# Reordering the opening of a two-layer convolution and feed-forward kernel, and splitting its last store

## The chip, the cores and the metric

One core of a Trainium2 chip, each group of runs on one chip. The engines are named as the profile names them: PE does the matmuls (PEld its weight loads), DVE is the vector engine, ACT the scalar engine, POOL the GpSimd engine, and SP the engine that issues most transfers (DMA); PSUM is the memory into which PE writes its results. The time is the device time of one launch in microseconds (us); a row of runs is given by its median. The profile's span is shorter than the time by a constant 1.8 us or so (353.4 against 355.2 for one run of the kernel before). A few runs of such kernels fall in a slower state, with a lower granted clock; all runs used here are of the fast state unless said otherwise. The kernel before took 355.32 us (354.15 to 355.44) before any of this.

## The reference, cut to what matters

```python
def A(q, k, v, shift_k, ssm_k, ssm_D):          # long convolution, S = 2048, D = 512
    k_shift = causal 4-tap filter of k per column, taps shift_k
    kv = k_shift * v
    y  = irfft(rfft(kv, 2S) * rfft(ssm_k, 2S))[:S]
    return q * (y + kv * ssm_D)
def B(x, w_gate, w_up, w_down):                 # F = 1792
    return (silu(x @ w_gate) * (x @ w_up)) @ w_down

x = q
for layer in range(2):
    x = x + A(layernorm(x), k, v, ...)
    x = x + B(layernorm(x), ...)
```

## The kernel before

The rows are cut into four chunks of 512. The Fourier transforms are matmuls with tables of sines (`fwd`, `inv`), `h` is the convolution's kernel `ssm_k`, and the four-tap filter is a matmul of the transposed `k` (`kTb`) with diagonal matrices of the taps (`dg`). One chunk's convolution runs among the feed-forward matmuls of the chunk ahead of it. To that end every operation is first put on a list, with engine, estimated cost and buffers; a planner orders the list, and the program is then emitted in that fixed order. An engine runs its own operations strictly in that order.

```python
SLK = 9.39                                      # constants that steer the planner; some 15 of them, tuned together
ST1 = lambda l, c, h: (l, c, h) in {(0, 2, 0), (0, 3, 1), (1, 0, 1)}   # which statistics go to ACT
...
def add(self, eng, cost, emit, r=(), w=(), lat=None, due=None, ...):   # one operation for the planner
...
    for o in seq:                                # emission, in the planned order
        ...                                      # warming matmuls fill the planned wait at the start:
        n = int((start - t - 0.4) / 0.085)
        o.emit()
...
    load_k(0, -70)                               # on ACT
    ... tapR ...                                 # on SP
    load_h(0, "ACT", -59)                        # second on ACT
    load_v(0, -59); load_x(0, -58)               # on SP
    # a tiny copy makes the gate weights wait for h:
    add("POOL", 0.1, lambda: nc.gpsimd.tensor_copy(out=wt["g"].t[0:1, 0, 0:1], in_=hn[0].t[0:1, 0, 0:1]), ...)
    wg = load_weights("g", -57)
    load_h(1, "SP", -56.5, after=[wg]); load_k(1, -56.4, after=[wg])
    load_weights("u", -56, after=[wg]); load_weights("d", -55, after=[wg])
    ...
    for n in range(2):                           # inverse tables: 14 PE transposes, 2 ACT copies
        for i in range(NI):
            nc.tensor.transpose(it.t[:, i, :], fwd.t[:, n * NI + i, :], ident.t[:])
    ...
    v1 = load_v(1, ...)                          # the second chunk's v, on SP, into the one buffer of the first
```

## Time and profile before

| | before |
|---|---|
| first useful matmul | 7.18 us |
| first feed-forward matmul | 35.94 us |
| end of the last matmul | 350.11 us |
| end of the span | 353.4 us |
| PE waits after the first useful matmul | 0.2 us, once |

A feed-forward matmul is one with `pf` or `pd` as output. The time can be read as three stretches: up to the first useful matmul; the opening, from there to the first feed-forward matmul; and the main part, to the last matmul. In the last two PE works almost without a break (the view of waits leaves out gaps under 0.15 us). The view of waits for PE of the kernel before has one entry besides the start (engine, output, line, what it waited for: total us, times, longest us):

```profile
PE pf L335 <- ACT sg L838: 0.2, 1, 0.2
```

The second `v` was issued at 24.81 us, landed 8.0 us later, and the first product with it ran on DVE at 41.7 us.

### The profile page before, as it was taken

Reading aid. Unit: us, or ns where it says so; the run is one execution under the profiler, and the core shown is the slowest. Engines: PE = TensorE matmul, PEld = TensorE weight load, DVE = VectorE, ACT = ScalarE, POOL = GpSimd, SP = SyncE. Lnnn points to the kernel's source line nnn. Section 1 sums busy time; section 2 is a strip of 40 time slices with the busy share of each in tenths; the row PEclk is TensorE's granted clock in tenths of the full one; section 3 lists DMA queues with packets and bytes.
Section 4 is the critical chain, followed back from the end, with each engine's and each line's share of the span. In section 5 each row is a group of like instructions: output and inputs, shape, how many; then the busy total and the mean of one; then the engine's idle time right before and its main releaser. Section 6 shows DMA issues by size and latency. Waiting matters only on the chain.

```text
span 353.4 us, 6784 instructions
## 1 busy us (share of the span) xinstructions
PE 347.8 (98%) x2716; PEld 254.9 (72%) x2716; DVE 276.4 (78%) x511; ACT 249.6 (71%) x470; POOL 38.2 (11%) x42
## 2 busy tenths in 40 slices
PE   7999999999999999999999999999999999999996
PEld 7745976867777686858677676758687777778673
DVE  4997999999989999999997999799973323545111
ACT  4768684859897865758869994946488975646452
POOL 1001010111102110111220010201111000001000
PEclk9999999999999999999999999999999999999999
DMA  6999230010343222012101033010101010101100
GB/s 238 289 340 312 49 88 3 2 30 2 71 109 76 77 89 32 0 32 60 32 32 31 14 107 61 0 32 1 32 30 32 30 32 1 24 7 24 37 2 30
DMA packets 37897, 21.98 MB, mean 62 GB/s; under 512 B 29797, under 2 KB 35690, under 8 KB 37866
## 3 DMA queue, kind: packets, MB, share of 16 engines
q1 hardware_dynamic: 37192, 20.51, 22.0%
q10 hardware_dynamic: 674, 1.05, 0.9%
q8 instruction: 21, 0.34, 0.4%
q14 instruction: 10, 0.08, 0.1%
HBM read 12.33 MB, written 2.10 MB: 41 GB/s over the span
## 4 chain that ended last, share of the span: by engine, by line
PE 65%; DVE 26%; ACT 4%; issue 2%; POOL 2%; ACTq 0%; DVEq 0%; POOLq 0%
PE pf L335 36%; PE pd L852 18%; PE ps L335 8%; DVE ht L845 3%; DVE bnst L707 3%; DVE m L519 2%; DVE t L636 2%; DVE t L652 2%; DVE t L642 2%; ACT H L424 2%; DVE Z L657 2%; PE wm L1024 2%; DVE G L556 1%; DVE xc L778 1%; POOL rstd L712 1%
## 5 line engine op out<-in xcount | busy, mean ns | idle before, releaser
L335 PE MATMUL pf<-zT,wg_sb 128*128 128x256 bf16 x896 | 116.1, 273 | 0.2 <-ACT sg L838 0.2
L335 PE MATMUL pf<-zT,wu_sb 128*128 128x256 bf16 x896 | 116.1, 273 | 0.0
L852 PE MATMUL pd<-wd_sb,ht 128*128 128x512 bf16 x448 | 103.1, 379 | 0.0
L335 PEld LDWEIGHTS <-wg_sb 128*128 128x128 bf16 x896 | 87.6, 98 | 19.4 <-issue 0.5
L335 PEld LDWEIGHTS <-wu_sb 128*128 128x128 bf16 x896 | 87.6, 98 | 11.4
L838 ACT ACTIVATE sg<-pf 128x512 bf16<-128x512 f32 x112 | 67.5, 603 | 26.1 <-PE pf L335 25.9
L842 ACT CAST ht<-pf 128x512 bf16<-128x512 f32 x112 | 66.0, 590 | 18.7 <-PE pf L335 18.1
L852 PEld LDWEIGHTS <-ht 128*128 128x128 bf16 x448 | 43.8, 98 | 47.1
L845 DVE TENSOR_TENSOR ht<-ht,sg 128x1024 bf16<-128x1024 bf16 x64 | 39.3, 618 | 33.4 <-ACT ht L842 33.4
L712 POOL TENSOR_TENSOR rstd<-ve,nhalf 128x2 f32<-128x2 f32 x25 | 29.1, 1163 | 207.0 <-DVE ve L710 185.8
L707 DVE BATCH_NORM_STATS2 bnst<-xc 128x6 f32<-128x512 bf16 x50 | 32.2, 683 | 0.5
L864 ACT CAST dn<-pd 128x512 bf16<-128x512 f32 x26 | 13.9, 589 | 25.1 <-PE pd L852 25.1
L636 DVE TENSOR_TENSOR t<-X,G 128x2048 bf16<-128x2048 bf16 x18 | 21.9, 1218 | 0.0
L642 DVE TENSOR_TENSOR t<-X,G 128x2048 bf16<-128x2048 bf16 x18 | 21.9, 1217 | 0.0
L871 DVE TENSOR_TENSOR xc<-xc,dn 128x1024 bf16<-128x1024 bf16 x13 | 8.9, 687 | 15.9 <-ACT dn L864 15.8
L424 ACT ACTIVATE X<-ps 128x512 bf16<-128x512 f32 x32 | 18.6, 605 | 2.0 <-PE ps L335 1.9
L751 ACT ACTIVATE z<-xc,nmr,rstd 128x512 bf16<-128x512 bf16 x18 | 13.6, 807 | 2.7 <-DVE nmr L744 2.6
L737 POOL TENSOR_TENSOR rstd<-ve,nhalf 128x2 f32<-128x2 f32 x7 | 7.8, 1117 | 70.5 <-DVE ve L733 70.5
L335 PE MATMUL ps<-vt,fwd 128*128 128x512 bf16 x56 | 15.2, 379 | 0.0
L335 PEld LDWEIGHTS <-fwd 128*128 128x128 bf16 x96 | 9.3, 98 | 7.9 <-issue 0.2
L652 DVE TENSOR_TENSOR t<-t,t 128x2048 bf16<-128x2048 bf16 x12 | 14.7, 1221 | 0.1
L657 DVE TENSOR_TENSOR Z<-Z,t 128x2048 bf16<-128x2048 bf16 x12 | 14.7, 1221 | 0.1
(96 smaller groups left out, 317.6 us busy)
## 6 DMA issues: line engine op xcount, KB each, us to landing
vt<-in_A_v_dram SPq DMA_DIRECT2D x4, 512.0 KB, 4.0
xc<-in_A_q_dram SPq DMA_DIRECT2D x4, 512.0 KB, 4.9
out_dram<-xc SPq DMA_DIRECT2D x16, 128.0 KB, 1.8
wg_sb<-in_B_w_gate_dram SPq DMA_DIRECT2D x1, 1792.0 KB, 7.7
wu_sb<-in_B_w_up_dram SPq DMA_DIRECT2D x1, 1792.0 KB
wd_sb<-in_B_w_down_dram SPq DMA_DIRECT2D x1, 1792.0 KB, 13.4
hn<-in_A_ssm_k_dram SPq DMA_DIRECT2D x3, 512.0 KB, 6.3
kn<-in_A_k_dram ACTq DMA_DIRECT2D x1, 512.0 KB, 3.5
```

The source lines that it names most:

```text
L335: nc.tensor.matmul(o, lhsT=lhsT, rhs=rhs, start=(n == 0), stop=(n == len(terms) - 1))
L424: add("ACT", act(D), lambda: nc.scalar.activation(out=view(), in_=ps.t[:], func=ACT.Copy, scale=scale), r=[ps], w=[(buf, keys)], conv=conv)
L636: dve(n * D, lambda t1=t1, part=part: nc.vector.tensor_mul(out=t1.t[:], in0=x.t[:, sl, 0, :], in1=g.t[:, sl, part, :]), [(x, key(slots, (0 ...
L642: dve(n * D, lambda t2=t2, part=part: nc.vector.tensor_mul(out=t2.t[:], in0=x.t[:, sl, 1, :], in1=g.t[:, sl, 1 - part, :]), [(x, key(slots ...
L652: dve(n * D, lambda t1=t1, t2=t2, comb=comb: nc.vector.tensor_tensor(out=t1.t[:], in0=t1.t[:], in1=t2.t[:], op=comb), [t2], [t1], conv=conv)
L657: dve(n * D, lambda t1=t1, part=part: nc.vector.tensor_add(out=z.t[:, sl, part, :], in0=z.t[:, sl, part, :], in1=t1.t[:]), [t1], [zk], con ...
L707: add("DVE", 0.6, lambda st=st, i=i: nc.vector.bn_stats(out=st.t[:], in_=xs[c].t[:, i, :]), r=[(xs[c], (i,))], w=[st])
L712: add("POOL", PW, lambda: nc.gpsimd.tensor_tensor(out=rstd.t[:], in0=ve.t[:], in1=nhalf.t[:].to_broadcast((P, n)), op=ALU.pow), r=[ve, nha ...
L838: add("ACT", act(D), lambda ps=ps, o=o, sg=sg: nc.scalar.activation(out=sg.t[:, o:o + 2, :], in_=ps.t[:], func=ACT.Silu), r=[ps], w=[(sg, ...
L842: add("ACT", act(D), lambda ps=ps, o=o, ht=ht: nc.scalar.copy(out=ht.t[:, o:o + 2, :], in_=ps.t[:]), r=[ps], w=[(ht, (o // 2,))], due=(uni ...
L845: dve(n * W, lambda sg=sg, ht=ht: nc.vector.tensor_mul(out=ht.t[:], in0=ht.t[:], in1=sg.t[:]), [sg], [ht], due=(unit, k / pairs, 0.0, "h"))
L852: nc.tensor.matmul(pds[o].t[:], lhsT=ht.t[:, q, o * P:(o + 1) * P], rhs=wt["d"].t[:, ft, :], start=(ft == 0 and not xpe), stop=(ft == NF - 1))
```

## The change

The intent is to start PE's useful work earlier. The first `h` becomes the first transfer of ACT's queue, alone there. The other loads stand in one line on SP, and the gate weights no longer wait for `h`. The filter of `k` is done by column groups, so that it can start on a part; half of the spectrum of `h` comes ahead of it. The statistics and normalisation of the first rows move from DVE to ACT. The inverse tables are made by two transposing DMA loads in place of PE. The last row's result is copied and stored in two halves on two queues. All planner constants were tuned anew. The core of the diff, with cuts:

```diff
-SLK = 9.39
+SLK = 8.59
 ...                                             (all planner constants)
-                            n = int((start - t - 0.4) / 0.085)
+                            n = int((start - max(t, 1.0) - 0.3) / 0.106)
 ...
-    load_k(0, -70)
+    load_h(0, "ACT", -70)
 ...
-    add("POOL", 0.1, ... tensor_copy(out=wt["g"]..., in_=hn[0]...))
-    wg = load_weights("g", -57)
+    k0 = load_k(0, -69)                          # now on SP
+    v0 = load_v(0, -59, after=[k0])
+    x0 = load_x(0, -58, after=[v0])
+    wg = load_weights("g", -57, after=[x0])
+    for n in range(2):
+        tabs = add("SP", 2.2, lambda sl=sl: nc.sync.dma_start_transpose(
+            out=inv.t[:, sl, :], in_=fwd.t[:, sl, :].rearrange("p k f -> p (k f)")), ...)
+    load_h(1, "SP", -56.5, after=[tabs])
+    load_k(1, -56.4, after=[tabs])
+    load_weights("u", -56, after=[tabs])
+    load_weights("d", -55, after=[tabs])
-    for n in range(2):
-        ... nc.tensor.transpose(it.t[:, i, :], fwd.t[:, n * NI + i, :], ident.t[:])
 ...
+            for half_, (eng, cs) in enumerate((("DVE", slice(0, D // 2)), ("ACT", slice(D // 2, D)))):
+                add(eng, 0.35, ... copy of half a row ...)
+                q, qn = (nc.scalar, "ACT") if half_ else (nc.sync, "SP")
+                add(qn, 0.4, ... q.dma_start(out=o_t[:, c, i, cs], in_=x.t[:, i, cs]) ...)
```

## The prediction

> **What bounds the kernel now.** I first cut the span into stages, with the busy time of each engine in each. The columns are busy microseconds and, in brackets, instructions; then granted clock, the share of the DMA engines, GB/s.
>
> ```profile
> 0.00:1.72 1.72, 0.00 (x0) 0.00 (x1) 0.59 (x4) 0.00 (x0) 1.02 (x9) 1.00 0.01 1
> 1.72:7.05 5.33, 5.33 (x51) 5.23 (x52) 2.39 (x11) 2.52 (x4) 0.11 (x1) 1.00 0.97 358
> 7.05:17.70 10.65, 10.35 (x133) 8.16 (x132) 10.08 (x24) 7.74 (x17) 0.88 (x2) 1.00 0.83 259
> 17.70:24.80 7.10, 7.10 (x34) 3.23 (x33) 7.10 (x16) 5.26 (x10) 0.00 (x0) 1.00 1.05 335
> 24.80:35.94 11.14, 11.03 (x81) 6.16 (x80) 9.12 (x25) 9.04 (x17) 1.48 (x2) 1.00 1.13 317
> 35.94:349.71 313.77, 313.60 (x2423) 232.16 (x2421) 247.09 (x438) 223.96 (x423) 34.72 (x29) 1.00 0.15 36
> 349.71:353.40 3.69, 0.40 (x2) 0.00 (x0) 0.00 (x0) 1.07 (x2) 0.00 (x0) 1.00 0.21 71
> ```
>
> The order is PE, PEld, DVE, ACT, POOL. PE is busy almost without a gap from 1.72 us to the end of the matmuls. A busy PE need not be a fast PE, so I checked its pace in the chain that ended last (start, length, what):
>
> ```profile
> 313.14 10.48 PE pf L335 x96
> 327.09 4.32 PE pd L852 x20
> ```
>
> That is 10.48/96 = 0.109 us for a 256-column matmul and 4.32/20 = 0.216 us for a 512-column one. From 35.94 us on, the kernel owes 1792 of the first kind (195.7 us) and, by the counts of the groups, 448 + 6 + 24 + 24 + 16 = 518 of the second (111.9 us), and 112 shift matmuls of 128 columns at about 0.0585 us (3.73 us for 64 in the opening) make 6.6 us. The sum, 314.2 us, is the length of that stage: from the first feed-forward matmul on, PE has nothing to give back. The change can gain only ahead of it and behind it, or by taking work off PE.
>
> Ahead of it, PE's own work by group is 88 matmuls of 512 columns (19.0 us), 150 of 128 (8.8 us) and the four tap transposes (0.3 us): 28.1 us, in the 28.9 us from 7.05 to 35.94. So this stretch too is full but for some 0.8 us. The part that is not work is the beginning. The timeline there (start, length, engine, line, what) reads:
>
> ```profile
> 0.73 0.39 ACTq L364 DMA_DIRECT2D kn<-in_A_k_dram  x1
> 1.15 0.48 ACTq L359 DMA_DIRECT2D hn<-in_A_ssm_k_dram  x1
> 1.72 5.40 PE L1024 MATMUL wm<-ident 128*128 128x128 bf16 x51 [1.72 <-POOL ident masks.py:199]
> 7.18 0.27 PE L929 MATMUL pt<-ident,tapR 4*128 4x4 bf16 x4
> 7.37 1.07 PE L379 MATMUL pt<-ident,kn 128*128 128x128 bf16 x16
> 8.62 0.39 SPq L402 DMA_DIRECT2D wg_sb<-in_B_w_gate_dram  x1
> ```
>
> The 51 matmuls of wm are throwaway warming. They run 0.106 us apart (5.40/51), but the plan that counted them assumed 0.085, so they hold PE in program order until 7.13 us. The first block of k had landed 3.5 us after its issue by the transfer view, at about 4.2 us, nearly 3 us earlier. The first h, second on its queue and among four loads of 512 KB, took 7.2 us and landed at 8.35.
>
> **What the Trainium skill says.** "TensorE: Matmul & The Clock Gate", Part 1, says that PE starts at half clock, reaches full clock only after a busy window of about 3.4 us that runs freely (so the moment varies), and that 128-column matmuls come 107 ns apart cold and 56 ns warm. The trace agrees: 106 ns for wm, 314 ns each in duration until the end of that block, then 219 ns for the transposes of k. The granted-clock column reads 1.00 all along and does not show this. "DMA: Bandwidth & Descriptors", section "Issuing engines are not separate DMA queues", says that loads issued from two engines share the same 16 DMA engines and interleave; its "Queues, rings and completion order" says that each DMA engine takes turns between queues. The trace agrees: share 0.97 and 358 GB/s over 1.72 to 7.05, with h slowest of the four. So a queue of its own gives h no new bandwidth, but it is first there and then gets its turn against k alone. "Trainium Kernel Development and Optimization", Performance Expectations, warns that matmul busy time says little of the distance to the limit; hence the pace check above.
>
> **The change part by part.**
> First h on its own queue: issued at about 0.73 us as the first ACT transfer. What stood in that place took 3.5 us, so h lands near 4.2; its rows are shorter and k joins after 0.8 us, so I take 4.5 and PE's first useful transpose at 4.6. The warming count is now divided by 0.106 and so no longer overruns. PE starts 7.05 - 4.6 = 2.45 us earlier.
> What is lost of it: in the trace PE was still cold until 7.1 us. The warming starts at the same 1.7 us, so the useful work from 4.6 to about 7.1 runs at half pace and gets 1.25 us of work done in 2.5. Some of that would be waiting for the copies out of PSUM anyway; I charge 1.0 us.
> Loads in one line: k, v, x, then the gate weights without the wait for h (6.6 us on POOL, issue at 8.62). DMA no longer pauses around 8 to 10 us. The gate weights landed 7.7 us after issue, near 16.3, and are needed at 35.9, so this is off the path and only makes room for the table transposes.
> Inverse tables by DMA: 14 PE transposes go, 14 x 0.0585 = 0.82 us of a full PE, with two ACT copies (1.73 us, not on the path). Two DMA transposes come in; the 128x512 ones took 2.4 us to land, so 128x896 ones some 4 us (estimate, by size). Behind the gate weights they land before about 18 us; the first inverse matmul was at 24.62 and will be near 21.5. Hidden.
> Shift by column groups, half of the h spectrum first, statistics of the first rows on ACT: no PE work changes, only its order. DVE loses four batch statistics (4 x 0.68, their aggregates 4 x 0.17, two small ones 0.34), four normalisations (1.63), one dg block (0.69) and the drow add (0.41), about 6.5 us, and gets eight small operations (1.3), two copies out of PSUM (1.3) and a memset (0.2), some 2.8. So it is 3.7 us lighter. The moved residual adds take another 2 x 0.69 from it in the second row block and return them in the third. ACT gains about 7 us in all. It has room: 250 us busy of 353. New waits between shorter pieces I set at 0.8 us, equal to the slack already there: 0.
> The last row in halves: now PE ends at 350.11 and the second ACT copy at 350.78. A half copy of 256 columns is about 0.35 us (estimate: 0.58 for 512 and 0.93 for 896 give 0.92 ns an element), so 0.44 in place of 0.67, and a 64 KB store in place of 128 KB saves at most 0.1. Together 0.3 us. Thirteen groups of last-row matmuls have twice the instructions at half the columns: 0.218 for 0.216, nothing.
> Sum: -2.45 + 1.0 - 0.82 + 0 - 0.3 = -2.6 us, 352.7 us.
>
> **The rivals.**
> One: the clock costs nothing, because the window happens to end early or the cold time lies under waits; then -3.6 us and 351.7, and with the old 0.8 us of slack gone 351. For it: the warm-up moment varies. Against it: 5.3 us of warming were needed in this trace.
> Two: DVE becomes the bound. It is 98% busy from 36 to 180 us (for example 19.73 of 20 us in 60 to 80), and the chain runs on DVE from 101.9 to 206 us. PE idled only 0.17 us there, so the two are level. If DVE cannot move forward by as much as PE, PE waits near 205 us and the gain is cut there. For it: the tie. Against it: DVE is lighter by 5 us ahead of that point, more than PE's 2.6. If it fails: 354 to 355.
> Three: the opening starves. The up and down weights come behind more transfers on the one line and the sync engine is held by a transpose load for 7.85 us. The down weights landed at 31.5; they would be needed at about 36.8. Five us late and the gain is gone: 355 or more. I hold that unlikely, because the gate weights start earlier.
> Four: the shift chain (taps, dg, k copies, products with v) sets the pace, so that the earlier h spectrum only moves the same idle time to 8 to 14 us: gain about 1.5 us, 354.
>
> **Range and chances.** The floor is start 4.6, 28.1 - 0.8 of opening work, 313.8, and a tail of 3.4: 349.9 of span, plus the 1.9 by which the time exceeded the span (355.32 against 353.4), or 351.8; an h at 4.2 and no gaps give 351.4. The three runs spread over 1.3 us. So 8 in 10 lie in 350.9 to 354.4. Faster by over 2% means under 348.2, below that floor: 3%. Slower by over 2% would need the opening broken: 1%.
>
> **What would show it.** Right: in the profile of after, the first transposes of h between 4.2 and 5 us with 300 ns durations; few wm; the first feed-forward matmul near 33.6 us; PE full from there with the same two paces; the inverse tables landed before 20 us; a tail after the last matmul near 3.0 us. Wrong: PE gaps over 1 us in 6 to 33, a pf matmul waiting for weights, or PE idle near 100 or 205 us behind DVE. A first feed-forward matmul under 32 us would mean that the opening held more slack than I counted.

## The result, and the profile after

The kernel after took 354.94 us (354.51 to 355.37, 6 runs) beside 355.21 us (354.15 to 355.45, 6 runs) of the kernel before. The ratio is 0.9996, with a 95% interval of 0.9981 to 1.0011. Here and below a ratio is the mean time of one kernel's fast runs over that of the kernel before's of the same rounds, so it is not quite the ratio of the medians. The change is worth nothing measurable. The prediction was 352.7 us with a range of 350.9 to 354.4, so the forecast gain did not come, and the time lies just above the range.

The stages of after, cut at its own landmarks (first useful matmul 4.29, first feed-forward matmul 35.10, copies out from 349.13; columns as in the prediction's first view):

```profile
0.00:1.72 1.72, 0.00 (x0) 0.00 (x1) 0.81 (x5) 0.55 (x1) 1.02 (x9) 1.00 0.01 2
1.72:4.29 2.57, 2.57 (x24) 2.37 (x24) 2.22 (x10) 1.94 (x4) 0.11 (x1) 1.00 0.92 313
4.29:17.70 13.41, 13.41 (x135) 9.51 (x135) 11.90 (x26) 10.61 (x25) 4.14 (x5) 1.00 1.09 301
17.70:24.80 7.10, 7.10 (x46) 3.70 (x45) 6.24 (x14) 6.11 (x10) 0.00 (x0) 1.00 1.06 329
24.80:35.10 10.30, 8.99 (x95) 6.20 (x94) 5.97 (x15) 7.94 (x17) 0.69 (x1) 1.00 1.14 359
35.10:349.13 314.03, 312.18 (x2391) 231.18 (x2391) 249.07 (x444) 220.43 (x420) 37.91 (x30) 1.00 0.16 36
349.13:353.00 3.87, 0.40 (x4) 0.11 (x2) 0.42 (x1) 0.86 (x2) 0.00 (x0) 1.00 0.23 68
```

The start is 2.89 us earlier, yet the first feed-forward matmul is only 0.84 us earlier. In the stage before it PE is busy for 8.99 of 10.30 us, and in the main part for 312.18 of 314.03, where it had been busy for 313.60 of 313.77. The pace is what it was, as the chain that ended last shows (start, length, what):

```profile
312.52 12.23 PE pf L335 x112
324.75 6.04 PE pd L877 x28
```

That is 12.23/112 = 0.109 us and 6.04/28 = 0.216 us. So PE lost time to waits, not to pace. The opening itself went as planned at first (the timeline: start, length, engine, line, what):

```profile
0.72 0.43 ACTq L359 DMA_DIRECT2D hn<-in_A_ssm_k_dram  x1
...
1.72 2.63 PE L1066 MATMUL wm<-ident 128*128 128x128 bf16 x23 [1.72 <-POOL ident masks.py:199]
...
4.29 0.29 PE L980 MATMUL pt<-ident,tapR 4*128 4x4 bf16 x4
...
4.51 1.71 PE L481 MATMUL pt<-ident,hn 128*128 128x128 bf16 x16
```

`h` landed 3.5 us after its issue, there are 23 warming matmuls in place of 51, and the first 13 of the 16 transposes of `h` start up to 107 ns apart, at half pace, until 5.9 us; after that the transposes start 56 ns apart. Against that warm pace PE lost 0.65 us there. (Expectations below put this at 0.84 us. The time up to 8 us gives that only if the four tap transposes, 0.22 us, are counted as lost too.) What came later is in the waits of PE, of which there is now this list:

```profile
PE pf L335 <- ACT zT L817: 1.3, 1, 1.3
PE pf L335 <- DMA zT<-z: 1.0, 1, 1.0
PE pd L877 <- DVE ht L864: 0.5, 1, 0.5
PE pf L335 <- ACT sg L857: 0.4, 1, 0.4
```

The first lies at 33.8 to 35.1 us, the others at 77.2, 235.0 and 148.7 us. They sum to 3.2 us against 0.2 before. The timeline around the first says where it comes from:

```profile
32.97 0.76 DVE L513 TENSOR_TENSOR vt<-ks,vt 128x512 bf16<-128x512 bf16 x2 [2.39 <-DMA vt<-in_A_v_dram]
...
33.49 0.59 ACT L512 CAST ks<-ps 128x512 bf16<-128x512 f32 x1 [2.30 <-DVE vt L513]
...
33.97 1.08 ACT L817 COPY zT<-ptz 128x512 bf16<-128x512 bf16 x2
...
35.10 1.03 PE L335 MATMUL pf<-zT,wg_sb 128*128 128x256 bf16 x8 [1.31 <-ACT zT L817]
```

DVE stood 2.39 us for the second `v`. ACT's next copy of filtered `k` (`ks`) needed the buffer that this product frees, and stood 2.30 us. The copies that feed the first feed-forward matmul (`zT`) are behind it on ACT, so PE stood 1.31 us. The second `v` had been issued on SP at 21.08 us, behind the up weights (18.43) and the down weights (19.05), 1.8 MB each, and landed 11.77 us later; the issue itself held SP for 3.92 of these. It could not be issued much earlier, because it goes into the buffer of the first `v`, which PE reads until 21 us. The planner had moved its use from 41.7 to 30.6 us and its issue only from 24.81 to 21.08 us.

Why so much earlier? In the kernel after, 128 shift matmuls (`dg` with `kTb`) lie ahead of the first feed-forward matmul, where there were 80, and 28 inverse ones in place of 32. The tuned order does most of the second chunk's filter in the opening.

A balance of the two spans. A 128-column matmul counts 0.056 us here, the start-to-start time. The opening lasts 30.81 us in place of 28.76, and holds 1.0 us more work (48 x 0.056 - 4 x 0.216 - 14 x 0.056), so its losses grew by 1.0: 0.65 of cold pace, 1.31 of waiting and 0.2 of small gaps, in place of some 1.2 of small gaps before. The main part lasts 314.43 us in place of 314.17, with 1.8 us less work, so its losses grew by 2.1, of which 1.7 are in the list (1.9 in place of 0.2). The tail adds 0.13. With the start at -2.89 and the table transposes at -0.78 the sum is -0.4, and the spans differ by 0.45. The late `v` and the waits of the main part are thus the two causes to test.

### The profile page after: what moved, and what is told of

The parts are those of the page before. It is cut to its first block, busy times and chain, and to the rows that moved or that the text cites. A ratio compares the mean times of both kernels' runs of the same rounds, so it can differ in the third digit from the quotient of the medians.

```text
span 353.0 us, 6745 instructions
## 1 busy us (share of the span) xinstructions
PE 344.6 (98%) x2688; PEld 253.1 (72%) x2688; DVE 276.6 (78%) x511; ACT 248.4 (70%) x474; POOL 43.9 (12%) x45
## 4 chain that ended last, share of the span: by engine, by line
PE 55%; DVE 31%; DMA 4%; ACT 3%; issue 3%; POOL 3%; DVEq 0%; POOLq 0%; ACTq 0%
PE pf L335 32%; PE pd L877 16%; DVE ht L864 4%; PE ps L335 4%; DMA vt<-in_A_v_dram 3%; DVE bnst L720 3%; DVE m L532 3%; DVE t L655 3%; DVE t L665 2%; DVE t L649 2%; PE ps L462 2%; DVE Z L670 2%; POOL rstd L725 2%; DVE n L790 1%; DMA zT<-z 1%
## 5 line engine op out<-in xcount | busy, mean ns | idle before, releaser
L877 PE MATMUL pd<-wd_sb,ht 128*128 128x512 bf16 (+1 forms) x462 | 100.8, 373 | 0.5 <-DVE ht L864 0.5
L877 PEld LDWEIGHTS <-ht 128*128 128x128 bf16 x462 | 45.1, 98 | 49.0 <-DVE ht L864 1.4
L861 ACT CAST ht<-pf 128x512 bf16<-128x512 f32 x112 | 66.4, 593 | 14.7 <-PE pf L335 13.8
L725 POOL TENSOR_TENSOR rstd<-ve,nhalf 128x2 f32<-128x2 f32 x24 | 28.6, 1192 | 194.9 <-DVE ve L723 179.5
L720 DVE BATCH_NORM_STATS2 bnst<-xc 128x6 f32<-128x512 bf16 x48 | 31.1, 685 | 0.5
L750 POOL TENSOR_TENSOR rstd<-ve,nhalf 128x2 f32<-128x2 f32 x8 | 11.1, 1386 | 80.0 <-DVE ve L746 80.0
L423 ACT ACTIVATE X<-ps 128x512 bf16<-128x512 f32 x32 | 17.8, 608 | 4.3 <-PE ps L335 3.0
L764 ACT ACTIVATE z<-xc,nmr,rstd 128x512 bf16<-128x512 bf16 x16 | 12.1, 806 | 4.2 <-DVE nmr L757 4.2
L790 DVE TENSOR_TENSOR n<-n,Yk 128x1024 bf16<-128x1024 bf16 x15 | 10.4, 692 | 4.3 <-ACT n L764 3.7
L423 ACT ACTIVATE H<-ps 128x512 bf16<-128x512 f32 x24 | 13.5, 638 | 0.0
## 6 DMA issues: line engine op xcount, KB each, us to landing
wd_sb<-in_B_w_down_dram SPq DMA_DIRECT2D x1, 1792.0 KB, 12.5
```

Of the source, the lines that this page charges most:

```text
L423: add("ACT", act(D), lambda: nc.scalar.activation(out=view(), in_=ps.t[:], func=ACT.Copy, scale=scale), r=[ps], w=[(buf, keys)], conv=conv)
L720: add("DVE", 0.6, lambda st=st, i=i: nc.vector.bn_stats(out=st.t[:], in_=xs[c].t[:, i, :]), r=[(xs[c], (i,))], w=[st])
L725: add("POOL", PW, lambda: nc.gpsimd.tensor_tensor(out=rstd.t[:], in0=ve.t[:], in1=nhalf.t[:].to_broadcast((P, n)), op=ALU.pow), r=[ve, nha ...
L861: add("ACT", act(D), lambda ps=ps, o=o, ht=ht: nc.scalar.copy(out=ht.t[:, o:o + 2, :], in_=ps.t[:]), r=[ps], w=[(ht, (o // 2,))], due=(uni ...
L877: nc.tensor.matmul((pds[o] if not cs.start else pds[HP]).t[:, cs], lhsT=ht.t[:, q, o * P:(o + 1) * P], rhs=wt["d"].t[:, ft, cs], start=(ft ...
```

## The experiments

Fifteen runs were made, in four groups, some of them repeats; each group shares its runs of the kernel before (medians 354.70, 354.96, 354.72 and 354.84 us, 11 runs each). All gave correct results. "Runs" lists median and range.

### Second v ahead of the down weights

```diff
-        plan.issue(*plan.order(PASSES), 32.0, warm)
+        seq, place, when = plan.order(PASSES)
+        seq.remove(wd)                           # wd: the load of the down weights
+        seq.insert(seq.index(v1) + 1, wd)
+        plan.issue(seq, place, when, 32.0, warm)
```

> After, with one issue moved on the sync engine: the down weights go out behind the second v block instead of ahead of it. No other engine's order changes. My theory: v then lands near 27 us instead of 32.85, the 2.4 us that DVE waited for it and the 1.3 us that PE waited before its first feed-forward matmul (35.10) vanish, that matmul comes near 33.7, and the later PE waits (1.0 at 77 us, 0.4 at 149, 0.5 at 235), which come of a late DVE, shrink to under 1 us in sum. Time 352.2 to 353.4. Rival one, DVE is the bound from 36 to 235 us anyway: the first matmul moves but the later PE waits grow by as much; 354.5 or more. Rival two, the DMA line is full whatever the order: the down weights are then late and PE waits for them at 40 to 46 us; 355 or more.

Runs: 354.05 us (353.73 to 354.44), ratio 0.9982 (0.9968 to 0.9995). The second `v` landed 6.8 us after its issue and DVE waited for it no more. The down weights came later without anyone waiting for them. The three main waits stayed (0.8, 0.5 and 0.4 us). The time is less of a gain than the theory had (352.2 to 353.4), and the first feed-forward matmul came at 34.61 us, not 33.7. In this profile PE stayed at half pace up to 7.8 us, which cost 1.5 us where the profile of after had lost 0.65; `k` landed at 6.3 us, 0.6 later, but PE stood only some 0.1 us for it.

### Second v on ACT's queue

```diff
-        return add("SP", 0.6, lambda: nc.sync.dma_start(out=vt[b].t[:], ...
+        return add("SP", 0.6, lambda: (nc.scalar if b == 1 else nc.sync).dma_start(out=vt[b].t[:], ...
```

> After, with the second v block issued from the scalar engine, on the other queue; the order of the other engines is kept. My theory: it takes turns with the up and down weights instead of waiting behind them, lands near 26 to 28 us, and the gain is that of the run with the down weights behind v: 352.2 to 353.4. Rival, DMA bandwidth and not the line order sets its landing: it lands near 31 to 33 as before and the time stays at 355.

Runs: 353.57 us (352.92 to 353.90), ratio 0.9966 (0.9952 to 0.9979). `v` landed 7.4 us after its issue at 21.2, which held ACT for 0.35 us only; the up and down weights took 8.8 and 13.8 us, where they had taken 7.4 and 12.5. The first feed-forward matmul came at 33.76 us. The waits of PE in the main part of this run:

```profile
PE pf L335 <- DMA zT<-z: 0.8, 1, 0.8
PE pd L877 <- DVE ht L864: 0.5, 1, 0.5
PE pf L335 <- ACT sg L857: 0.4, 1, 0.4
```

The wait of 1.3 us is gone; the other three stay, and merely come 1.6 us earlier. The time is a little above the 353.4 us that the theory gave at most. So the late `v` is one cause, and it is not the cause of the rest.

### Inverse tables on PE again

```diff
-        tabs = add("SP", 2.2, lambda sl=sl: nc.sync.dma_start_transpose(out=inv.t[:, sl, :], ...
+        for i in range(NI):
+            nc.tensor.transpose(it.t[:, i, :], fwd.t[:, n * NI + i, :], ident.t[:])
+        ... two ACT copies into inv; the loads behind come straight after the gate weights
```

> After, with the inverse tables made by 14 PE transposes and two ACT copies again, all else of the change kept (the order after 4 us is planned anew). My theory: the two DMA transposes held the sync engine for 7.6 us and the DMA engines for some 2 to 3 us; without them the weights and the second v land 2 us earlier, DVE waits under 1 us for v, and that outweighs the 0.8 us of PE work: 353.8 to 354.8. Rival, the tables by DMA were free and gained what I predicted: 355.6 to 356.

Runs: 354.71 us (354.43 to 355.92), ratio 1.0006 (0.9990 to 1.0022), beside 0.9996 for after in its own rounds. The order was planned anew for it. DVE waited 1.0 us for the second `v` in place of 2.39, PE's waits were 0.6 and 0.2 us, and the first feed-forward matmul came at 33.88 us. What the DMA tables save PE (0.82 us by the prediction) is not visible in the time, which lies where the theory had it. In after the two issues hold SP for 4.35 and 3.18 us, and the loads behind them come later: the second `h` was issued at 12.45 us, in before at 9.05 and in this run at 3.58. How much of the outcome is this and how much the new order, this run cannot tell.

### Last row in one piece

```diff
-    LAST_UNIT = (1, NB - 1, HP - 1)
+    LAST_UNIT = None
```

> After, with the last row finished and stored whole as in before; only the last unit differs. In the trace of after the end lies 3.47 us behind the last matmul, in before 3.29. My theory: the halves gained nothing at the end; this run ends about 3.3 us behind its last matmul, time 354.6 to 355.1, level with after. Rival, the predicted gain of 0.3 us by the halves is there and hidden by something else: 355.2 to 355.4 and a tail of 3.6 to 3.8.

Runs: 355.25 us (354.66 to 357.62), ratio 1.0027 (1.0003 to 1.0051). The profile is of the slowest of these runs, in which DVE waited 3.15 us for `v` and PE 2.28, and the clock fell behind that wait, as shown for the next run. So the time of this one run is mostly the late `v`; for the other five, which have no profile, that is not shown. The tail from the last matmul to the end of the span was 3.37 us, against 3.45 with halves: no loss.

### The control, and each kernel with the other's constants

First after as it is, then the kernel with `v` on ACT's queue with the constants of before, then before with the constants of after:

```diff
-SLK = 8.59
+SLK = 9.39
 ... (and the other planner constants; the third run has this the other way round, on the kernel before)
```

> The changed kernel itself, as a control beside the others on this chip. Its ratio to before was 0.9996 in its own rounds. I expect 0.998 to 1.001, a DVE wait for the second v block of 1 to 3 us (it differs from run to run with the DMA line), and the same three PE waits at 76, 148 and 234 us, some 1.0, 0.4 and 0.5.

Runs: 355.56 us (354.64 to 356.73), ratio 1.0016 (0.9998 to 1.0034). The profiled run was a long one, 356.60 us: DVE waited 3.1 us for `v`, and PE 2.28 at the first feed-forward matmul, where the first profile had 2.39 and 1.31. The wait for `v` differs from run to run, by about 1 us in these two. And it had a second cost. Right behind the wait of 2.28 us the granted clock was 0.50 for 3.41 us, as the view by windows shows for PE (window, its length, busy us and instructions, granted clock, DMA share, GB/s):

```profile
35.00:36.00 1.00, 0.25 (x3) 1.00 0.38 36
36.00:37.00 1.00, 1.00 (x8) 0.52 1.27 287
37.00:38.00 1.00, 1.00 (x6) 0.50 0.55 126
```

The feed-forward matmuls started 213 ns apart in place of 109, and PE lost 1.67 us of pace. The profile of the run with the last row whole, with the same wait, shows the same (3.41 us at 0.50, again 1.67 us lost). Behind the wait of 1.31 us in the first profile of after the clock stayed at 1.00. Of the six runs here the two longest, 356.60 and 356.73 us, have a mean granted clock of 0.993, the other four 0.999 or 1.000.

> The version with the second v block on its own queue (ratio 0.9966), with the planner's constants of before (slacks, durations, stretches, the choices of engine for statistics and normalisation). It tells why PE still waits some 1.9 us in sum at 75, 147 and 233 us, although v now comes in time. Theory, those waits are built into the order that the new constants give: with the old ones they are gone or under 0.5 in sum, and the ratio falls to 0.991 to 0.994. Rival, with PE 2 us earlier DVE can't follow in any order: waits of 1.5 us or more remain, in other places, and the ratio stays at 0.996 or rises.

Runs: 355.51 us in the five fast ones (354.58 to 355.82), ratio 1.0012 (0.9998 to 1.0026). The gain that the theory forecast for the old constants (a ratio of 0.991 to 0.994) did not come: the ratio is higher than with the new ones (0.9966). The profiled run was of the slow state (365.42 us, clock 0.949), so whether the three waits were gone in it is not known.

> The kernel before with the planner's constants of after, nothing else. Theory, the waits come of the order that the new constants give: PE, which waited 0.2 us in the whole feed-forward part, now waits 1 us or more and the ratio is 1.002 to 1.006. Rival, the constants are harmless and only the earlier start of PE brings waits: PE waits under 0.5 us and the ratio is 0.999 to 1.001.

Runs: 356.63 us (355.92 to 357.00), ratio 1.0044 (1.0030 to 1.0057). PE waits of 0.6, 0.4 and 0.2 us came up in a kernel that had 0.2. Each kernel is worse with the other's constants: a set of them fits the kernel it was tuned on.

### Warming: earlier, and none

```diff
-                            n = int((start - max(t, 1.0) - 0.3) / 0.106)
+                            n = int((start - max(t, 0.4) - 0.3) / 0.106)
...
-            nc.tensor.matmul(t[:], lhsT=ident.t[:], rhs=ident.t[:], start=True, stop=True)
+            nc.tensor.matmul(t[:], lhsT=wz.t[:], rhs=wz.t[:], start=True, stop=True)   # wz is set by DVE, ready at 1 us
```

> The version with v on its own queue, with the warming matmuls on a tile that DVE sets at the very start, so that they begin near 1.1 us and not at 1.72, and six more of them. Theory, the 0.84 us that the first transposes and matmuls lost to the cold clock shrinks with every tenth of earlier warming: full clock by 5.5 us, loss 0.2 to 0.6, ratio 0.9950 to 0.9962. Rival, the moment at which the clock rises is set by a free-running window: the loss stays at 0.5 to 1.5 us, whichever way it falls, ratio 0.996 to 0.998.

Runs: 352.60 us (352.07 to 353.21), ratio 0.9934 (0.9922 to 0.9946), beside 0.9966 without. It looked like a gain, but not the one expected: the matmuls at half pace lost 0.49 us in this profile and 0.33 in the profile without (the expectations' 0.98 and 0.84 count other gaps up to 8 us too), so the loss was no smaller. So it ran again, next to its own control, to the same edit:

> The version with the second v block on its own queue, a repeat beside the early warming on one chip. Ratio 0.9966 before; I expect 0.995 to 0.998, a first feed-forward matmul near 33.8 us, and PE waits of 0 to 1.0 us near 75 us for the transposed z (3.8 us between z and PE's need of it, so it depends on the DMA of that run).

Runs: 353.69 us (352.96 to 354.32), ratio 0.9965 (0.9952 to 0.9979), as the first time.

> The version with v on its own queue and warming from about 1.1 us, a repeat. Its ratio was 0.9934 against 0.9966 without the early warming, but in other rounds, and its profile showed no smaller loss to the cold clock (0.98 against 0.84 us). Theory, the early warming is worth something on average: at least 0.002 under the repeat without it in these same rounds. Rival, the difference was the run's luck (the 1 us wait for z at 75 us): the two ratios within 0.0015 of each other.

Runs: 353.19 us (352.99 to 355.12), ratio 0.9962 (0.9943 to 0.9981). The gain of the first time did not come again; two series on two chips do not agree, and no gain is shown. Nor did the full pace come sooner: it came at 4.8 to 6.7 us in the six profiles of this document whose warming starts at 1.04 us, and at 5.2 to 7.8 us in the nine of the fast state that start at 1.72, with a median of 6.0 us in both. Then the opposite, on the kernel with `v` on ACT's queue: no warming at all.

```diff
-                            if n > 0:
+                            if n > 0 and t > 1.0:
```

> The version with v on its own queue without any warming matmuls, to measure the cold clock by itself. Theory: PE's first useful work at 4.3 us then runs at half pace until a busy window has passed, some 3.5 to 7 us, so the loss rises from 0.8 to 2 to 3 us and the ratio to 1.000 to 1.004. Rival, the opening waits for copies and loads anyway and hides the cold clock: the ratio stays within 0.001 of the version with warming.

Runs: 353.50 us (353.12 to 354.60), ratio 0.9963 (0.9949 to 0.9978), beside 0.9965 with warming. The ratio did not rise as expected. The profiled run is the slowest of its six. In it PE waits for the taps (2.18 us) and then for `h` (1.89 us), and runs at half pace up to 9.8 us, which lost 2.4 us. There the first feed-forward matmul came at 35.71 us, 1.4 later than in the control's profile, and the wait at 76 us was gone, so that the span was longer by 1.0 only (352.8 against 351.8). That a late opening is in part taken up by that wait is one reading of one profile. The six times together show no difference; by the two intervals, one of more than some 0.7 us is ruled out, a smaller one is not.

### Early warming and the last row whole

Both edits above on the kernel with `v` on ACT's queue.

> The early-warming version with the last row whole, so that the halves are measured where no wait for v blurs the runs. Theory, the halves gain nothing: ratio within 0.001 of the early-warming version's, tail behind the last matmul 3.3 to 3.4 us against 3.4 to 3.5. Rival, the halves gain the predicted 0.3 us or more: ratio higher by 0.001 to 0.003 (the earlier run with the whole tail read 0.003 higher than after).

Runs: 353.02 us (352.09 to 353.62), ratio 0.9947 (0.9933 to 0.9962). The tail was 3.37 us, against 3.44 with halves in the same group. The ratio is 0.0015 under that of the early-warming version (0.9962), not within 0.001, but the intervals overlap and the rival had it higher. So no gain of the halves is shown. The transfer view of after shows why (issues, KB each, median us from issue to landing):

```profile
out_dram<-xc SPq DMA_DIRECT2D x15, 128.0 KB, 1.8
...
out_dram<-xc ACTq DMA_DIRECT2D x1, 64.0 KB, 1.8
```

The store of half the size whose landing the view gives lands no sooner. And the last store on SP, the first half of the last row, was issued at 350.17 us, because SP had the other row's store to issue at 349.74 and an issue holds it for some 0.4 us; its data had been ready at 349.77. From the last matmul to the last issue it was 0.64 us with halves and 0.70 us before (350.81 - 350.11).

### The three main waits, each with its own place in the order

Left open was whether these waits belong to three places of the planned order, or to DVE and ACT being full (DVE is busy for 19.79 of 20 us from 60 to 80 us), so that any order has them. In the trace each waiting matmul leads back to one short operation that stood behind longer ones on an engine that keeps its order. The kernel of the run above was planned as it is, and then eight operations were moved by a few places:

```diff
-        plan.issue(*plan.order(PASSES), 32.0, warm)
+        seq, place, when = plan.order(PASSES)
+        for n, to in ((438, 308), (441, 309),                            # near 66 us, DVE: ve, nmr before t, t
+                      (819, 793), (820, 793), (821, 822), (789, 821),    # near 144 us, ACT: n, n behind sg, ht
+                      (1175, 1020), (1182, 1020)):                       # near 231 us, DVE: ht, ht before X, X
+            o, b = next(q for q in seq if q.n == n), next(q for q in seq if q.n == to)
+            seq.remove(o); seq.insert(seq.index(b), o)                   # o goes ahead of b
+        plan.issue(seq, place, when, 32.0, warm)
```

> The fastest version so far (second v on its own queue, early warming, last row whole) with eight of its operations moved by a few places in the fixed order, all else as planned: at 66 us the variance of the next row block and its small product go ahead of two large shift products on DVE; at 144 us two half normalises on ACT go behind the sigmoid and copy that free the feed-forward accumulators; at 231 us two gate products on DVE go ahead of two spectrum additions. Theory (the re-planned order itself puts each of these three late operations behind longer ones on a full engine, and that is all of the 1.9 us of PE waits): the three waits fall from 1.9 to under 0.6 us, and the time by about 1.3 us, ratio near 0.991. Rival (DVE and ACT have no room, so the work that was moved back makes a later operation late): the waits move elsewhere and still sum to 1.5 us or more, ratio near 0.995 as before.

> As the run above, with only the two DVE moves at 66 us. Theory: the wait of PE for the transposed rows near 76 us (0.5 to 0.9 us) goes, the other two (0.4 and 0.5) stay; ratio 0.5 to 0.9 us lower, near 0.993. Rival: that wait is set by how long the transposing load takes to land, which differs from run to run, and it stays or turns up with the same size elsewhere; ratio near 0.995.

> The control of the two runs above: the same kernel as the fastest version of the run before (second v on its own queue, early warming, last row whole), unchanged. Both theories: ratio 0.9947 as then, give or take 0.0015; PE waits of 0.5 to 0.9 us near 76, 0.4 near 147 and 0.5 near 233 us.

| | runs, us | ratio (95% interval) | PE waits in the main part |
|---|---|---|---|
| all three places | 351.97 (351.53 to 352.42) | 0.9920 (0.9908 to 0.9932) | 0.3 |
| the first alone | 352.33 (352.21 to 352.94) | 0.9934 (0.9922 to 0.9945) | 0.4, 0.4, 0.2 |
| control | 353.41 (353.13 to 353.48) | 0.9957 (0.9945 to 0.9969) | 0.7 in two, 0.5, 0.3 |

What moved, on DVE near 67 us; first the control, then with all moves:

```profile
66.44 1.22 DVE L655 TENSOR_TENSOR t<-X,G 128x2048 bf16<-128x2048 bf16 x1
67.57 0.16 DVE L746 TENSOR_SCALAR ve<-sm 128x2 f32<-128x2 f32 x1
...
68.24 1.22 DVE L665 TENSOR_TENSOR t<-t,t 128x2048 bf16<-128x2048 bf16 x1
69.38 0.15 DVE L757 SCALAR_TENSOR_TENSOR nmr<-mv,rstd 128x2 f32<-128x2 f32 x1
```

```profile
66.34 0.17 DVE L746 TENSOR_SCALAR ve<-sm 128x2 f32<-128x2 f32 x1 [0.23 <-ACT jk L742]
66.42 1.22 DVE L655 TENSOR_TENSOR t<-X,G 128x2048 bf16<-128x2048 bf16 x1
...
68.22 0.16 DVE L757 SCALAR_TENSOR_TENSOR nmr<-mv,rstd 128x2 f32<-128x2 f32 x1
68.30 1.22 DVE L665 TENSOR_TENSOR t<-t,t 128x2048 bf16<-128x2048 bf16 x1
```

The two operations of 0.16 us, on which ACT's normalisation of the next rows depends, come 1.2 us earlier, and the long products next to them move by less than 0.1. Near 144 us it is ACT; again first the control, then with all moves:

```profile
143.54 0.59 ACT L861 CAST ht<-pf 128x512 bf16<-128x512 f32 x1 [0.28 <-PE pf L335]
145.44 1.52 ACT L764 ACTIVATE n<-xc,nmr,rstd 128x512 bf16<-128x512 bf16 x2 [1.31 <-DVE nmr L757]
146.87 0.57 ACT L857 ACTIVATE sg<-pf 128x512 bf16<-128x512 f32 x1
```

```profile
144.20 0.59 ACT L861 CAST ht<-pf 128x512 bf16<-128x512 f32 x1 [0.28 <-PE pf L335]
144.68 1.52 ACT L764 ACTIVATE n<-xc,nmr,rstd 128x512 bf16<-128x512 bf16 x2
146.10 0.58 ACT L857 ACTIVATE sg<-pf 128x512 bf16<-128x512 f32 x1
```

In the control ACT stands 1.31 us for `nmr`, with the sigmoid (`sg`) that frees an accumulator behind the two normalisations (`n`); with the moves a sigmoid and a copy (`ht`) go first, and ACT does not stand. Near 231 us it is DVE: the two products `ht` start at 233.00 and 234.28 us in the control, and one behind the other from 231.21 with the moves. The wait list of the kernel with all moves has one entry left in the main part, at 156 us, a new place:

```profile
PE pf L335 <- DMA zT<-z: 0.3, 1, 0.3
```

The theory expected the waits to fall below 0.6 us and a ratio near 0.991; the rival, a ratio of 0.995 and waits of 1.5 us or more. It is 0.992 and 0.3 us, and the interval does not touch that of the control. Of the 1.7 us between the two profiled spans 1.3 lie in the main part and 0.4 in the opening, which the moves do not touch. The waits belong to places in the order, and full engines have room enough to be rid of them.

For the first place alone the account is less clean. The ratio fell by 0.0023, some 0.8 us, as expected. But in the control's profile the wait for `zT` was only 0.3 us (0.5 and 0.9 in the profiles of two runs before), so only 0.1 us of the gain can be seen there; another 0.2 is a second wait for `ht` that is gone. Of the 1.3 us between the two profiled spans (351.7 and 350.4) 0.5 lie in the opening, which the edit does not touch. How the gain of this step alone is made up stays open. From the first feed-forward matmul to the end of the last matmul it is 314.3 us in the control, 313.6 with the first place and 313.0 with all three.

With 351.97 us against 354.84 of its rounds, this version beats both kernels, by 0.8%.

## Why the prediction was wrong

**The start and the clock (-2.45 and +1.0).** Right in kind and nearly in size: useful work began at 4.29 us, not 4.6 (so -2.89), and the trace shows 0.65 us of cold pace, not 1.0. Warming or none made no difference to the time that these runs resolve, though, so the cold term has a size in the trace and none seen in the outcome. The reading behind it was a little off: in before the full pace came at 6.7 us, ahead of the end of the warming, not at its end.

**"No PE work changes, only its order", and "loads in one line".** The first step that failed. The prediction priced the second chunk's filter where it had been. In after, 48 more shift matmuls lie in the opening (some 2.7 us at 0.056), and with them the first use of the second `v`, 11 us earlier. It asked of the loads only whether the weights come in time (and there put the need of the down weights at 36.8 us, where before first uses them at 46.68); it never followed the second `v`, whose issue waits for its buffer and then for its turn behind 3.6 MB of weights. That wait cost 1.3 us in one profile and 2.3 in two others, where the half clock behind it cost 1.67 more. With `v` on ACT's queue the first feed-forward matmul came at 33.76 and 34.30 us, where the prediction said 33.6. That this fits is chance. The prediction missed 1.8 us of work (48 shift matmuls more, 4 inverse ones fewer). In the profile with 33.76 us that is offset by a start 0.3 earlier, 0.7 less of cold pace (0.33 for 1.0), and some 0.7 less of small gaps. The third rival, an opening that starves behind the weights, was the right place with the wrong transfer.

**"Waits at 0.8 us, equal to the slack already there: 0", and "PE full from there".** The second step that failed. The main part lost 1.9 us in three waits, each from the place of a short operation behind longer ones. The prediction took the kernel after to be as well tuned in its main part as the one before, on the ground that DVE would be lighter, by 3.7 us. It was not: DVE was busy for 276.63 us in place of 276.36. The prediction passed over the constants at the top of the diff: ST2, N_ACT and Z_ACT each lose an entry, and DVE gets back two batch statistics and four normalisations (48 for 50 and 36 for 36 in the traces, where it had reckoned with four fewer of each). And a lighter DVE does not help a small operation that stands behind a long one. The second rival had DVE as the bound near 205 us; the waits came at 77, 149 and 235 us, and not from DVE's total load, as undoing them by moves alone shows. Undone, with `v` in time, the kernel takes 351.97 us (with early warming and the last row whole). The prediction had named 351.8 as the floor, but its terms add up to 349.1 of span and 351.0 of time, so this match is chance too.

**Inverse tables by DMA (-0.82, hidden).** PE's 14 transposes went (0.78 us: the prediction's 0.0585 us a piece counts the last matmul's full length; the chain that ended last gives 0.056, and with it the opening before had some 1.2 us of slack, not 0.8). But putting them back costs nothing measurable (1.0006 beside 0.9996). They were to land before 20 us, and did, at 16.3 and 17.1; but each took 11.4 and 7.9 us from its issue, not some 4, and the issues held SP for 7.5 us, which the prediction left out.

**The tail (-0.3).** Mis-sized: it measured +0.1. A store takes 1.8 us to land at either size, and SP issues two stores one after the other, so the last issue comes no sooner. The kernels with a whole last row show the same tail.

**The range.** It was narrow at the top, 354.4, because every unknown was set to the slack of the old order. The rivals that would have widened it (354 to 355, 355 or more) were both partly true, and were given little weight. The fourth did not come: from 4.29 to 17.70 us PE was busy for 13.41 of 13.41 us.

## What to carry to other kernels

When a change plans an order anew, follow every operation whose use moved to the transfer that feeds it: when may it be issued, and what stands before it in its line. Compare the list of waits of before and after first; it names the places, and a full engine that keeps its order can still be rid of a wait by letting a short operation go ahead of a long one. Try a surprising gain again, next to its control, before building on it.

## What the Trainium skill lacked or had wrong

- "DMA: Bandwidth & Descriptors", "Issuing engines are not separate DMA queues", says that starting transfers from several engines saves only the sequencer's time to start them, usually small beside the transfer. Here that time was not small: the issue of the second `v` held SP for 3.92 us behind the weights and ACT for 0.35, and from its end `v` landed 7.9 and 7.1 us later. The ratio fell from 0.9996 and 1.0016 to 0.9966 and 0.9965. The weights took longer (8.8 and 13.8 us in place of 7.4 and 12.5).
- "TensorE: Matmul & The Clock Gate", Part 1, puts the cost of the ramp at under 1% of a typical span, and the trace agrees (0.65 us of 353). It does not say that warming matmuls may then be worth nothing: leaving them all out did not change the time (0.9963 beside 0.9965). Nor does it name a single wait this short as enough to bring the half clock back in the middle of a kernel: a wait of 2.28 us was followed by it in two profiles (3.41 us at 0.50, 1.67 us lost), one of 1.31 us in a third was not.
- No page says how long the issue of a DMA transpose of this size between two places in on-chip memory holds its engine; "DMA: Bandwidth & Descriptors" has only a cycle count for one of 8,192 tiles. Two of 128 x 896 held SP for 4.35 and 3.18 us, and landed 11.4 and 7.9 us after their issue.
- Nor does one say that a full engine may still be rid of waits by order alone: DVE was busy for 19.79 of 20 us, and eight operations moved by a few places took the ratio from 0.9957 to 0.9920.
